# DeltaNet and an MLP on one core: hidden products of two feature pairs made for both token halves at once, and the last chunk's diagonal blocks turned on chip

## The chip, the cores and the metric

The kernel runs on one core of a Trainium2 chip. The metric is the device time of one execution in microseconds. Before the change, three runs gave 632.87 us as their median (630.61 to 633.9).

Engines are named as in the profile: PE is TensorE's matmuls and PEld its weight loads, DVE is VectorE, ACT is ScalarE, POOL is GpSimd, SP is SyncE, which here issues DMAs.

## The reference

Two operators follow each other. The first is a recurrence over 768 tokens for each of 4 x 8 heads of 48 dimensions, with a 48 x 48 state; keys are normalised, and `y` reads the state before the token is added to it. The second is an MLP over 3072 tokens: 384 features to 2048, `h * sigmoid(h)`, and back to 384.

```python
k_n = k / (np.linalg.norm(k, axis=-1, keepdims=True) + 1e-06)
for t in range(S):
    y[:, :, t] = np.einsum('bhd,bhde->bhe', q[:, :, t], state)
    v_old = np.einsum('bhde,bhd->bhe', state, kt)
    state = state + bt[:, :, :, None] * np.einsum('bhd,bhe->bhde', kt, vt - v_old)
x = attn_out.transpose(0, 2, 1, 3).reshape(B * S, H * D)
h = x @ w_in
g = h * (1.0 / (1.0 + np.exp(-h)))
return g @ w_out
```

## The kernel before, in words

**Tiling.** The 768 tokens are worked on in six chunks of 128 (`c` = 0 to 5), each in two halves of 64 tokens (`hf`). The four batches lie in two groups `g`. A half chunk of all batches is one column tile of 4 x 64 = 256 tokens for the MLP, kept in `xTs[c, hf]` as three K tiles of 128 features. Every matrix product in FP32 is recorded as two MATMUL instructions and two weight loads.

**The recurrence.** For each chunk the kernel scores keys against keys and queries (`score`, L526), inverts triangular 64 x 64 matrices, and then advances the state. The inverse begins with the 32 x 32 diagonal blocks of all heads, four to a head: each partition holds one block (block row by column in the free dimension), so that DVE can eliminate in 31 steps (`invert`, L645), each a SCALAR_TENSOR_TENSOR (L656) and a TENSOR_TENSOR (L661). Scores come out with token rows on the partitions, so the blocks must be rearranged. For chunks 2 to 5 this goes through DRAM: `block_out` (L598) stores eight times on SP, `block_in` (L609) loads once, and after the inverse `low` and `up` are stored and read back in place by `read_up` (L617) into `xe`, `xi` and `crossed`. For chunk 1 it stays on chip: `diagonal_blocks` (L564) copies the blocks together, `turn_diagonal` (L576) transposes them on DVE, and `put_up` (L630) transposes the result twice and copies it in place. `merge` (L793) completes the inverses with small matmuls; `keys`, `inner`, `old`, `update` and `new` (L850 to L949) advance the state and make `y`; `even_heads` and `move` (L953, L923) bring `y` into `xTs`, by ACT copies and five DMAs on SP.

**The MLP.** `hidden(c, hf)` (L1081) makes the 2048 hidden features in eight rounds `f`; each round makes two feature blocks of 128 (six products of 256 columns), with one PSUM bank of the two in `M`, emptied by one Silu activation on ACT. `combine(c, hf)` (L1185) multiplies with `w_out` in a 2 x 2 x 2 scheme of seven products instead of eight (Strassen's, in Winograd's form): seven chains of eight products with 192 columns, for which DVE makes sums of hidden rows (`sum_g`, L1175: S1, S2, S3, S4). For the last chunk alone `hidden_of_both` (L1261) makes the hidden products of both halves at once, with such a seven-product scheme over two feature blocks, two of the three K tiles, and the two token halves. It uses all eight banks, sums of `w_in` (`sum_w_in`) and of the tokens (`sum_x`) made on DVE, copies of partial results by ACT, and adds on DVE.

**The order.** Nothing is left to a planner: `pin` (L78) chains each engine's instructions in the order in which the program emits them, and `in_line` (L92) does so for the DMAs on SP. The MLP of chunk c runs while the recurrence of chunk c+1 is prepared and solved: `pieces` is a generator of MLP work, and a text for each chunk (L1656) tells how it is crossed with the rest. In such a text `r` takes the next MLP step (three products of hidden rows, or four of a chain), `s` the next step of `solve(c)`, `y` the next step of `prepare(c + 1)` (queries turned by `turn_blocks`, scores, blocks out and in), `i` one step of the inverse, `g` the step sizes for it, `v` and `k` loads, `d` the waiting output stores, `m` the next chunk's key lengths. So an `i` between two `r` puts DVE's step between these MLP steps' DVE instructions.

## Time and profile before

| | us |
|---|---|
| three runs, median (lowest to highest) | 632.87 (630.61 to 633.9) |
| the profiled execution's own time | 633.96 |
| span of its trace | 631.8 |

The trace holds one execution. Its span is the time from the first to the last instruction; the execution's own time lies 2.2 us above it. "Busy" is the time in which an engine worked on at least one instruction. The chain that ended last follows the work back from the last instruction to what released each step; its rows give a start, a duration and what ran. In the view of the timeline and of the groups, a row has the engine, the line, the operation, output and inputs by the program's names, the shapes, a count, and then the durations; in brackets stands the idle time before it and what ended it. In the table of stretches a row has the limits, the length, the busy time of PE, PEld, DVE, ACT and POOL with the number of instructions, the granted clock of TensorE, the share of the DMA engines and GB/s. Rows that name a source line give the least, median and greatest duration in ns.

In this trace the MLP of chunk 4 begins at 455.7 us, its first combination at 482.9, its second half's hidden products at 501.1, and the second combination at 521.9; chunk 5's recurrence lies across the latter from 527 to 555. The last chunk's hidden products end at 591.9.

### The profile page before, as it was taken

The numbers are of one execution on the slowest core, as the hardware profiler recorded it, in microseconds if no ns is written. First come the engines' busy times: TensorE is split into PE (matmuls) and PEld (weight loads), VectorE is DVE, ScalarE is ACT, GpSimd is POOL, SyncE is SP. The second block draws the span as 40 slices with busy tenths as digits, with TensorE's granted clock in tenths as the row PEclk, the third lists the DMA queues.
The fourth block names the chain that finished last, engine by engine and source line by source line (L and its number), as shares of the span: only waits on it lengthen the run. The fifth ranks groups of instructions, "written<-read, shape, count | busy, mean of one in ns | idle before, by whom it ended". The sixth has DMA issues, their size and how long they took to land.

```text
span 631.8 us, 21374 instructions
## 1 busy us (share of the span) xinstructions
PE 617.7 (98%) x9390; PEld 543.3 (86%) x9390; DVE 415.5 (66%) x927; ACT 226.7 (36%) x516; POOL 94.0 (15%) x101
## 2 busy tenths in 40 slices
PE   8889989999999999999999999999999999999997
PEld 5578778666799989989989989989989989988997
DVE  6886779999667974546975554976444983345432
ACT  4657873332441122451122451122452122454210
POOL 5234631335020020020020010020002000000000
PEclk9869999999999999999999999999999999999999
DMA  9656506350459360459141359433254024010011
GB/s 175 134 141 199 170 16 149 116 86 4 101 100 186 62 108 4 95 107 188 34 92 20 72 125 156 65 75 44 52 113 95 2 75 62 17 38 1 0 26 26
DMA packets 136941, 52.61 MB, mean 83 GB/s; under 512 B 108672, under 2 KB 130432, under 8 KB 136848
## 3 DMA queue, kind: packets, MB, share of 16 engines
q1 hardware_dynamic: 136512, 51.09, 39.6%
q8 instruction: 74, 1.21, 0.9%
q10 hardware_dynamic: 336, 0.15, 0.1%
q14 instruction: 19, 0.16, 0.1%
HBM read 39.09 MB, written 9.96 MB: 78 GB/s over the span
## 4 chain that ended last, share of the span: by engine, by line
PE 93%; SPq 2%; DMA 1%; issue 1%; ACT 1%; DVE 0%
PE phid L1088 34%; PE px L1200 17%; PE py L1200 13%; PE po L1132 5%; PE pb_c L866 3%; PE pa L539 2%; SPq L144 2%; PE pb_c L1303 2%; PE pb_c L854 2%; PE pyc L945 2%; PE pc L1303 2%; PE pb_c L1132 2%; PE pb_c L886 2%; PE pa L1303 1%; PE pyc L932 1%; PE px L808 1%
## 5 line engine op out<-in xcount | busy, mean ns | idle before, releaser
L1088 PE MATMUL phid<-xT,w_in 128*128 128x256 f32 x960 | 214.9, 382 | 1.9 <-issue 1.7
L1088 PEld LDWEIGHTS phid<-xT,w_in 128*128 128x128 f32 x960 | 180.2, 190 | 26.9 <-issue 2.8
L1098 ACT ACTIVATE gT<-phid 128x512 f32<-128x512 f32 x72 | 42.9, 597 | 115.2 <-PE phid L1088 106.2
L656 DVE SCALAR_TENSOR_TENSOR rank<-g,step,x 128x31 f32<-128x31 f32 (+15 forms) x124 | 49.8, 402 | 23.3 <-DMA g<-blocks 19.8
L1200 PE MATMUL px<-sums_of_w,sums_of_g 128*128 128x192 f32 x320 | 56.6, 329 | 0.0
L1200 PE MATMUL py<-w_out,sums_of_g 128*128 128x192 f32 x320 | 56.2, 328 | 0.0
L1200 PEld LDWEIGHTS px<-sums_of_w,sums_of_g 128*128 128x128 f32 x320 | 52.2, 190 | 0.4
L1200 PEld LDWEIGHTS py<-w_out,sums_of_g 128*128 128x128 f32 x320 | 52.3, 190 | 0.3
L661 DVE TENSOR_TENSOR x<-x,rank 128x31 f32<-128x31 f32 (+15 forms) x124 | 42.5, 342 | 4.3
L477 POOL TENSOR_TENSOR vf<-vf,n_slot 128x768 f32<-128x768 f32 x10 | 14.8, 1492 | 175.4 <-DMA vf<-in_v_dram 129.9
L1183 DVE TENSOR_TENSOR sums_of_g<-gT 128x384 f32<-128x384 f32 (+1 forms) x48 | 24.6, 540 | 14.6 <-ACT gT L1098 14.5
L498 DVE STREAM_TRANSPOSE kq<-stage 128x512 f32<-128x512 f32 x28 | 28.4, 1121 | 6.8 <-DMA stage<-in_q_dram 3.5
L554 ACT COPY xT<-pyc 48x128 f32<-48x128 f32 (+2 forms) x120 | 31.1, 259 | 1.6
L1211 DVE TENSOR_TENSOR o<-o,kept 128x192 f32<-128x192 f32 (+1 forms) x29 | 11.5, 425 | 26.7 <-ACT kept L1208 26.7
L560 POOL COPY g<-x 64x256 f32<-64x256 f32 x4 | 5.0, 1244 | 150.8 <-DVE x L664 150.8
L891 DVE TENSOR_TENSOR state<-state,pb_c 128x384 f32<-128x384 f32 x22 | 11.2, 550 | 24.6 <-PE pb_c L886 24.6
L866 PEld LDWEIGHTS pb_c<-vf,xi 64*64 64x64 f32 x736 | 23.3, 138 | 3.2 <-issue 2.3
L866 PE MATMUL pb_c<-vf,xi 64*64 64x48 f32 x736 | 24.9, 223 | 0.1
L1132 PE MATMUL po<-w_out,gT 128*128 128x384 f32 x64 | 23.7, 491 | 0.0
L1200 PE MATMUL py<-w_out,gT 128*128 128x192 f32 x128 | 23.4, 331 | 0.0
L859 DVE TENSOR_TENSOR vf<-vf,pb_c 128x384 f32<-128x384 f32 x22 | 11.2, 550 | 18.3 <-PE pb_c L854 15.5
L1200 PE MATMUL px<-w_out,gT 128*128 128x192 f32 x128 | 22.4, 327 | 0.0
(293 smaller groups left out, 1094.5 us busy)
## 6 DMA issues: line engine op xcount, KB each, us to landing
vf<-in_v_dram SPq DMA_DIRECT2D x48, 96.0 KB, 2.8
out_dram<-o SPq DMA_DIRECT2D x42, 96.0 KB, 2.2
w_out<-in_moe_w_in_dram SPq DMA_DIRECT2D x4, 768.0 KB, 5.0
sums_of_w<-in_moe_w_out_dram SPq DMA_DIRECT2D x4, 768.0 KB, 4.6
kb<-in_k_dram SPq DMA_DIRECT2D x12, 192.0 KB, 4.5
kb<-in_k_dram SPq DMA_DIRECT2D x24, 96.0 KB, 4.0
raw<-in_moe_w_in_dram SPq DMA_DIRECT2D x3, 768.0 KB, 6.8
blocks<-ap SPq DMA_DIRECT2D x32, 64.0 KB, 1.9
```

The lines of the kernel that those rows point to most:

```text
L477: pin(nc.gpsimd.tensor_tensor(out=vf, in0=vf, in1=of, op=ALU.mult))
L498: pin(nc.vector.transpose(out=kqs[c, b][:, :, j, :].rearrange("p a (i m) -> p a m i", i=T), in_=src.rearrange("p a (m d) -> p a m d", d=D) ...
L554: return pin(nc.scalar.copy(to, of))
L656: pin(nc.vector.scalar_tensor_tensor(out=tv, in0=g[:, 0:m, m : m + 1].to_broadcast([P, m, n]), scalar=step[:, m : m + 1], in1=x[:, m : m + ...
L661: yield pin(nc.vector.tensor_tensor(out=x[:, 0:m, m:T], in0=x[:, 0:m, m:T], in1=tv, op=ALU.add))
L866: yield pin(nc.tensor.matmul(pz[rows, n * D : (n + 1) * D], lhsT=xis[g][rows, u * H + 2 * p + e, :], rhs=vfs[c][rows, hf, g * HB + u, p, : ...
L1088: pin(nc.tensor.matmul(ph[:, j * GT : (j + 1) * GT], lhsT=w_in[:, a, (2 * f + j) * P : (2 * f + j + 1) * P], rhs=xTs[c, hf][:, a, :], star ...
L1098: pin(nc.scalar.activation(out=hidden_of(c, hf, f), in_=ph[:], func=ACTF.Silu, scale=-0.5 if in_blocks(c) else 0.5))
L1132: pin(nc.tensor.matmul(pos[i][:, 0:DM], lhsT=hidden_of(0, hf, f // 2)[:, at : at + C], rhs=w_outs[f // HFF][:, f % HFF, :], start=(f == 0) ...
L1183: pin(nc.vector.tensor_tensor(out=sums_of_g[:, k, fs], in0=of[0], in1=of[1], op=op))
L1200: pin(nc.tensor.matmul(to, lhsT=at, rhs=quarter(f, *b) if isinstance(b, tuple) else sums_of_w[b][:, f], start=start and f == 0, stop=f == ...
L1303: pin(nc.tensor.matmul(to[:, i * GT : (i + 1) * GT], lhsT=left(a, slice(f, f + 1))[:, 0], rhs=right(b), start=start and i == 0 and n == 0, ...
```

## The change

For chunk 4 (the second last), the features' rounds 0, 1, 3 and 4 are taken as two pairs (0,1 and 3,4: `TWOS[:2]`), each made for both token halves at once by the scheme that the last chunk has already, which now is a class `Both` with its steps as methods. Rounds 2, 5, 6 and 7 (`PLAIN`) stay as they were, made by `plain`. `some_of_both` runs the four plain rounds of the first half, then the two pairs, crossed with each other, on the two banks of `M` and one each of `A` and `CC`, and the second half's round 7 between them; then comes the combination of the first half, then `others` with the second half's rounds 2, 5 and 6, then the second combination. The sums of `w_in` for the two pairs are made here, on DVE, behind the first two of the last chunk's four turned queries and ahead of the other two; they stay for the last chunk, which now makes only those of rounds 2, 5, 6 and 7 itself. The second half's hidden rows of the pairs lie in `kbufs[0]` and `stage`.

For chunk 5, the diagonal blocks no longer go through DRAM: they are copied into the end of `stage` by ACT (six copies) and DVE (two), transposed on DVE, and put in place after the inverse by two DVE transposes and ten copies (`put_up`), as chunk 1 has it: six by ACT, two each by DVE and POOL. POOL clears `spread` once, as the blocks of chunk 5 have another place in it. The texts for chunks 4 and 5 are written anew.

```diff
+        if c == NCH - 1:
+            pin(nc.gpsimd.memset(spread[:], 0.0))
...
-        return 2 * (1 - j % 2) + j // 2 if c > 1 else j
+        return 2 * (1 - j % 2) + j // 2 if 1 < c < NCH - 1 else j
...
-            room = stage if c == 0 else sum_room
+            room = (stage, sum_room, stage[:, -BH * T :])[min(c, 2)]
...
+    def put_up(c, x):
...
         pin(nc.vector.transpose(out=both[:].rearrange("p n s -> p s n"), in_=x))
-        up = work.tile([P, BH, T], FP32, name="up_1", tag="x", bufs=1)[:]
+        if c > 1:
+            yield
+        if c == 1:
+            up = work.tile([P, BH, T], FP32, name="up_1", tag="x", bufs=1)[:]
+        else:
+            up = zbuf[:, HB:B].rearrange("p b s a w -> p (b s a w)").rearrange("p (n t) -> p n t", t=T)
         pin(nc.vector.transpose(out=up.rearrange("p n t -> p t n"), in_=x.rearrange("p s t -> p t s")))
+        if c > 1:
+            yield
...
-        if c == 1:
-            put_up(x)
+        if c in (1, NCH - 1):
+            yield from put_up(c, x)
             return
...
+    ALONE = slice(2, NFF // 2, FG)
+    TWOS = [slice(f, f + 2) for f in range(0, NFF // 2, FG)]
+    PLAIN = [*range(NFF // 2)[ALONE], *range(NFF // 2)[TWOS[-1]]]
+
+    def groups_of(c, hf):
+
+        if (c, hf) == (LAST - 1, 1):
+            return [*TWOS, ALONE]
...
+    def plain(c, hf, f):
...
+    def sum_w_in(fs):
+
+        w = lambda which: block_in_w(which, fs)
+        yield by_in(w(S_1), w((1, 0)), w((1, 1)), ALU.add)
+        yield by_in(w(S_2), w(S_1), w((0, 0)))
+        yield by_in(w(S_4), w((0, 1)), w(S_2))
+        yield by_in(w(S_3), w((0, 0)), w((1, 0)))
...
+        def first(self, f):
+
+            self.chain_of[f] = at, a = self.take("pa")
+            yield from self.products(a, f, ((0, 0), (0, 0)), start=True)
+            by_act(self.place(f, 0, 0), halves_of(a))
+            tag, b = self.take("pb")
+            yield from self.products(b, f, ((0, 1), (1, 0)), ((0, 2), (2, 0)), start=True)
+            self.add(self.place(f, 0, 0), b)
+            self.late.append(self.place(f, 0, 0))
+            self.free.append(tag)
...
+        def sums(self, f):
+            p = self.p[f][1]
+            yield from self.products(p, f, (S_1, 1), start=True)
+            by_act(self.place(f, 1, 1), halves_of(p))
+
+        def second(self, f):
+
+            a = self.chain_of[f][1]
+            yield from self.products(a, f, (S_2, 2))
+            by_act(self.place(f, 0, 1), halves_of(a))
...
+        def rest(self, f):
+            yield from self.products(self.d[f][1], f, ((1, 2), (2, 1)), start=True)
+
+        def third(self, f):
+
+            a, to = self.chain_of[f][1], self.place(f, 1, 1)
+            yield from self.products(a, f, (S_3, 3))
+            for of in (a, self.d[f][1]):
+                self.add(to, of)
+            silu(self.c, to, to)
+            self.free.append(self.d.pop(f)[0])
+
+        def fourth(self, f):
+
+            to = self.place(f, 0, 1)
+            yield from self.products(self.p[f][1], f, (S_4, (1, 1)), ((0, 2), (2, 1)))
+            self.add(to, self.p[f][1])
+            silu(self.c, to, to)
+            self.free.append(self.p.pop(f)[0])
+
+        def last(self, f):
+
+            at, a = self.chain_of.pop(f)
+            yield from self.products(a, f, ((1, 1), 4), ((1, 2), (2, 0)))
+            silu(self.c, self.place(f, 1, 0), halves_of(a))
+            self.free.append(at)
...
+    def some_of_both(c):
+
+        turns = zbuf[:, 0:HB].rearrange("p b s a w -> p (b s a w)").rearrange("p (k t) -> p k t", k=4)
+        both = Both(c, M, turns)
+        one, two = (fs.start for fs in TWOS[:2])
+        for f in PLAIN:
+            if f <= FG * (NG - 1):
+                room_for(f // FG)
+            yield from plain(c, 0, f)
+            if f == TWOS[-1].start:
+                together(sum_w_in(TWOS[0]), sum_w_in(TWOS[1]), both.sum_x())
+            yield
+        for which in (S1, S2):
+            sum_g(c, 0, which, NG - 1)
+        yield from both.first(one)
+        rooms = A.popleft(), CC.popleft()
+        both.free.extendleft(rooms)
+        yield from both.first(two)
+        both.begin(one)
+        yield from both.sums(one)
+        yield from both.second(one)
+        both.outputs()
+        yield from both.rest(one)
+        yield from both.fourth(one)
+        yield from both.third(one)
+        both.begin(two)
+        yield from both.second(two)
+        yield from both.sums(two)
+        yield from both.last(one)
+        for which in (S1, S2):
+            sum_g(c, 0, which, 0)
+        yield from both.rest(two)
+        yield from both.fourth(two)
+        yield from both.third(two)
+        yield from plain(c, 1, PLAIN[-1])
+        yield
+        yield from both.last(two)
...
-            if b % HB == 1:
+            if b % HB == 1 and c < NCH - 1:
                 block_out(c, b // HB)
...
-            block_in(c)
+            if c == NCH - 1:
...
+                    diagonal_blocks(c, 0, (by_act, by_act) * 2)
...
+                diagonal_blocks(c, 1, (by_act, by_dve) * 2)
+                yield
+                turn_diagonal(c)
...
-        4: "s2 r4 s r2 s r s r2 s r s r2 s r3 s2 d v y r3 g y r3 y r2 y r6 i r i2 r i2 r i r i r i3 r i r i2 r k i r i r i2 r2 i r i r i2 r i r i r i3 r i r i2 r i r i r m i2 r m3 r m4 r m4 r m4 r m4 r m4 r m4 r m4 r m4 r m4 m99",
-        5: "r s r2 s r s r2 s r s r s r s r2 s r s r2 s",
+        4: "s2 r4 s r2 s r s r2 s r s r2 s r3 s2 d v y r3 g y r3 y r4 y i r2 i r i r i2 r i r i r i r2 i r i2 r i r i r i r i r i r i2 r i r i r i2 r i r i2 r i r i r i2 r i r i2 r i r2 i r3 i r2",
+        5: "r2 s r2 s r s r2 s r s r s r s r s r s r2 s",
...
+            elif c < LAST:
+                pieces = chained(pieces, some_of_both(c), combine(c, 0), others(c), combine(c, 1))
```

More of the change, by code (lines that the diff above doesn't have):

```diff
@@ L1219, in steps @@
                 yield
[L1221 removed]
+        gs = range(len(groups_of(c, hf)))
         yield from steps(
[L1223 removed]
+            chain(px[:, left], (0, 0), (0, 0), True), *((s, g) for s in (S1, S2) for g in (
+                gs[1:2] if (c, hf) == (LAST - 1, 0) else gs if (c, hf) in ((LAST - 1, 1), (LAST, 1)) else gs[-1:]
+            ))
         )
@@ new lines, in halves_of, with hidden_of_both, seconds @@
+    def halves_of(t):
+        return t[:].rearrange("p (f t) -> p f t", f=2)
+    def hidden_of_both(c):
+        both = Both(c, (*M, *CC, *A), stage[:, 3 * NFF // 2 * P :].rearrange("p (k t) -> p k t", k=4))
+        def seconds(*fs):
+            for f in fs:
+                both.begin(f)
+            for f in fs:
+                yield from both.sums(f)
+            for f in fs:
+                yield from both.second(f)
+            both.outputs()
+            for step in (both.rest, both.third, both.fourth, both.last):
+                for f in fs:
+                    yield from step(f)
+        yield from both.first(0)
+        yield from both.first(2)
+        together(both.sum_x())
+        together(sum_w_in(ALONE))
+        yield from both.first(4)
+        yield from seconds(0, 2)
+        together(sum_w_in(TWOS[-1]))
+        yield from both.first(6)
@@ L1377, in feed_forward, with others @@
+    def others(c):
+        room_for(0)
+        flush()
+        for f in PLAIN[:-1]:
+            yield from plain(c, 1, f)
+            yield
     def feed_forward(c, hf):
```

201 lines of the change are left out of this document (86 added, 115 removed).

## The prediction

> **What bounds the kernel now.** I read the page first, then the table of stretches, the list of waits, and the chain that ended last. The page says that TensorE is busy all through, at full granted clock after the first slices, and that it carries the chain.
>
> ```profile
> span 631.8 us, 21374 instructions
> ...
> PE 617.7 (98%) x9390; PEld 543.3 (86%) x9390; DVE 415.5 (66%) x927; ACT 226.7 (36%) x516; POOL 94.0 (15%) x101
> ...
> PEclk9869999999999999999999999999999999999999
> ...
> PE 93%; SPq 2%; DMA 1%; issue 1%; ACT 1%; DVE 0%
> ```
>
> A busy TensorE need not be one at its peak, so I asked for the stretches around the change: hidden products of chunk 4's first half up to the end of its combination (455.60 to 500.98), the rest of chunk 4 with chunk 5's recurrence (500.98 to 554.91), and the last chunk's products. The second view is of all that TensorE waited for from 380 us to the end.
>
> ```profile
> 455.60:500.98 45.38, 45.38 (x471) 41.89 (x467) 26.54 (x60) 13.69 (x37) 3.95 (x4) 1.00 0.41 85
> 500.98:554.91 53.93, 53.69 (x1049) 48.56 (x1047) 29.87 (x66) 16.35 (x40) 1.25 (x1) 1.00 0.25 45
> ```
> ```profile
> PE px L808 <- issue: 0.2, 1, 0.2
> PE pyc L945 <- issue: 0.2, 1, 0.2
> ```
>
> Only 0.4 us of idle in a quarter of a millisecond, and none of it for data. So the DRAM round trip of the last chunk's blocks, which the change takes away, is already free; only fewer TensorE instructions can shorten the time, and any new wait of TensorE lengthens it one for one. The chain gives the price of each:
>
> ```profile
> 404.81 20.72 PE phid L1088 x96
> ...
> 471.77 0.25 PE pa L539
> ...
> 473.68 9.26 PE phid L1088 x42
> ...
> 527.06 1.22 PE py L808 x82
> ...
> 533.65 0.65 PE px L808 x48
> 534.30 0.24 issue
> 534.54 0.77 PE px L808 x52
> 535.31 1.50 PE px L1200 x8
> 536.81 1.30 PE py L1200 x8
> ...
> 556.47 3.45 PE pb_c L1303 x16
> ```
>
> A product of 128x128 by 256 columns is two instructions. Plain ones cost 20.72/96 = 0.216 us each, those of the seven-product scheme 3.45/16 = 0.216 us: the same. Eight instructions of a chain cost 1.30 us, and 1.50 behind the small matmuls of the recurrence, so each return from these costs about 0.2 us.
>
> **The terms on TensorE.** A pair of rounds needs 2 x 6 products for each half of the tokens, 24 in all. In the new scheme a round's two feature blocks, two of the three K tiles and the two halves form a 2x2x2 product of seven instead of eight: 11 for a round, 22 for the pair. I count them in the steps: first 2+4, sums 2, second 2, rest 2, third 2, fourth 4, last 4. Two pairs (rounds 0,1 and 3,4) are so treated, which saves 4 products = 8 instructions = 8 x 0.216 = 1.73 us. Rounds 2, 5, 6, 7 stay plain. Walking through the two scripts, the recurrence still interrupts chunk 4's products at the same places, after 18, 36 and 54 instructions, and chunk 5's scripts cut the chains eight times as before (the first cut comes after 40 chain instructions instead of 32). So the number of 0.2 us returns does not change: 0. Chain instructions: 0.
>
> **The terms elsewhere.** Removed: eight block stores on SP, one load back, one POOL and one DVE copy, and the stores and loads of the inverse. SP's issues behind them are output stores that nobody awaits: 0 us. Added on ACT: twelve block copies, and for each pair three copies and four activations where four activations stood. Added on DVE: eight adds, twelve sums, three transposes, four copies; on POOL a memset and two copies. Their prices (L664 is the inverse's scaling; it stays):
>
> ```profile
> L554 ACT COPY stage<-ap 32x512 f32<-32x512 f32 x6 | 3.7, 615 | 0.1
> ```
> ```profile
> L664 DVE TENSOR_TENSOR x<-x,step 128x1024 f32<-128x1024 f32 x4 | 4.9, 1224 | 0.1
> ```
> ```profile
> L634 DVE STREAM_TRANSPOSE xe_y<-sums_of_w x1: 1958/1958/1958, 134.9 to 134.9; 128x1024 f32<-128x1024 f32 x1
> ```
> ```profile
> L560 POOL COPY xi<-up 32x512 f32<-32x512 f32 x2 | 1.6, 776 | 8.5 <-DVE up L636 8.4
> ```
> ```profile
> 559.77 0.42 DVE L1277 TENSOR_TENSOR stage<-xT 128x256 f32<-128x256 f32 x1
> ...
> 561.76 0.69 DVE L1277 TENSOR_TENSOR kq<-kq,pb 128x512 f32<-128x512 f32 x1 [0.43 <-PE pb L1303]
> ```
>
> ACT gets 12 x 0.615 = 7.4 us of block copies and six more copies of about 0.6, 11 us in all, over 70 us in which it worked 30 of 99. DVE gets 8 x 0.69 + 12 x 0.42 + 3 x 1.96 + 4 x 0.6 = 18.8 us. Both fit on average, so what counts is where TensorE stands behind one of them in order. There are three such places.
>
> **Place 1, the sums.** They are issued after 36 product instructions, so behind the first two turned queries and ahead of the other two, which now wait behind them; behind those stand the masks of the scores, and TensorE waits for turned queries and masks.
>
> ```profile
> 461.60 2.02 DVE L498 STREAM_TRANSPOSE kq<-stage 128x512 f32<-128x512 f32 x2
> 465.10 2.18 DVE L498 STREAM_TRANSPOSE kq<-stage 128x512 f32<-128x512 f32 x2 [1.47 <-DMA stage<-in_q_dram]
> 467.50 0.42 DVE L549 TENSOR_TENSOR ap<-pa,above 128x256 f32<-128x256 f32 x1 [0.22 <-ACT ap L554]
> ```
> ```profile
> 462.76 3.18 SPq L925 DMA_DIRECT2D xT<-part  x5
> ```
> ```profile
> xT<-part SPq DMA_DIRECT2D x3, 48.0 KB, 2.2
> ```
>
> Two weight sums fit in before the sum of the tokens' second half must wait for its moves: issued from 462.76 on, 2.2 us to landing in the table of DMA issues, so the first is there at about 465.2. Nine more operations at 0.42 end at 469.0, the two transposes (2.02) at 471.0. The scores that need them began at 471.77 in the chain, 18 product instructions after the other scores, and still do: margin 0.8 us, so 0. If the moves landed 1.5 us later, this place would cost 0.7.
>
> **Place 2, the crossing of pair one, pair two and the inverse.** The products of pair one and two use two to four PSUM banks, so TensorE waits for ACT's copy and DVE's add before a bank is used again. After 473.68 TensorE has 148 - 54 = 94 instructions left up to the combination, 20.3 us. Pair one's "rest" product comes 26 instructions in, at 473.68 + 0.20 + 26 x 0.216 = 479.5, and overwrites the bank that the add of pair two must have read. ACT must first finish the scores' copies, then make six block copies, then that pair's copy:
>
> ```profile
> 474.00 0.38 ACT L554 COPY ap<-pb_c 128x256 f32<-128x256 f32 x1
> ```
>
> 474.4 + 6 x 0.615 + 0.6 = 478.7, add to 479.4, and about 0.2 us from the hand-over and from the bank being needed when the instruction starts rather than ends. TensorE waits some 0.3 us. From then on DVE has the block transpose 1.96, seven adds at 0.69, the first eight steps of the inverse and two sums of the hidden rows at 0.55, in order between the adds:
>
> ```profile
> 486.07 0.27 DVE L656 SCALAR_TENSOR_TENSOR rank<-g,step,x 128x31 f32<-128x31 f32 x1 [1.58 <-DMA g<-blocks]
> ...
> 491.66 0.43 DVE L656 SCALAR_TENSOR_TENSOR rank<-g,step,x 128x207 f32<-128x207 f32 x1
> ```
>
> Eight steps took 491.66 - 486.07 = 5.6 us, so the sum is 1.96 + 4.83 + 5.6 + 1.1 = 13.5 us, and TensorE wants the last add at 473.88 + 86 x 0.216 = 492.5, which is 13.6 us after DVE began at 478.9. DVE is full here. Placing the adds one by one, two hand-overs have less than 0.1 us to spare (the third product's add before the last products of pair one; the copy before the fourth products of pair two); I give each 0.1 us. Waits: 0.3 + 0.2 = 0.5 us. Lower bound 0 (a wait can't be negative, and none goes away). Upper bound: each of the seven adds stands behind a whole step, in the first case behind the transpose:
>
> ```profile
> L656 DVE SCALAR_TENSOR_TENSOR rank<-g,step,x 128x31 f32<-128x31 f32 (+15 forms) x31 | 12.5, 402 | 2.5 <-DMA g<-blocks 1.6
> L661 DVE TENSOR_TENSOR x<-x,rank 128x31 f32<-128x31 f32 (+15 forms) x31 | 10.6, 342 | 1.1
> ```
>
> 7 x 0.83 (0.402 + 0.342 and two gaps of 0.04) + 1.96 = 7.8 us. I take the value near the lower end, since the steps here are the short first ones and the written order puts most of them behind an add.
>
> **Place 3, the end of the inverse.** It starts some 4.5 us earlier (behind the transpose at 481.5, instead of 486.07). On DVE stand then 31 steps of 0.83 (25.7), six of the adds (4.1), the hidden rows' and outputs' sums of the first half (about 6), the scaling 1.22: it ends at 518.6, the two transposes at 520.5 and 522.5, ACT's six copies behind them at 526.2. Chunk 5's recurrence needs the first transpose at 473.9 + 20.3 + 112 x 0.1625 + 36 x 0.216 + 40 x 0.1625 = 526.7, and the copies a good 6 us later: margins of 6 us, so 0. The eight sums for chunk 4's second combination stand behind the second transpose; the first four end at 522.5 + 4 x 0.42 = 524.2 and are wanted at 525.4.
>
> One row of before speaks to that margin: a sum of hidden rows took twice its 0.55 us while POOL scaled vf.
>
> ```profile
> 476.26 2.91 POOL L477 TENSOR_TENSOR vf<-vf,n_slot 128x768 f32<-128x768 f32 x2 [53.80 <-DMA vf<-in_v_dram]
> 479.10 0.95 POOL L592 MEMSET x<- 128x1024 f32 x1
> ```
> ```profile
> 478.43 1.15 DVE L1183 TENSOR_TENSOR sums_of_g<-gT 128x384 f32<-128x384 f32 x1 [2.48 <-ACT gT L1098]
> 479.61 0.56 DVE L1183 TENSOR_TENSOR sums_of_g<-sums_of_g,gT 128x384 f32<-128x384 f32 x1
> ```
>
> POOL's two new copies (2 x 0.78 us) start with the same transpose's end as those eight sums. The Trainium skill, page "SBUF — State Buffer", section "Who interferes with whom", says that a VectorE instruction with two SBUF inputs and a GpSimd instruction that reads SBUF share a port, and that the later of the two is held until the other has ended; the 1.15 agrees with it. By that rule the sums would be held for up to 1.55 us against a margin of 1.2, and the total would come out 0.35 us higher than by the row of an undisturbed sum; the adds of place 2 take one input from PSUM and would not be held. That lies inside the forecast's own range, so it gets no chance of its own.
>
> **The sum.** -1.73 + 0.5 = -1.2 us. The profiled execution took 633.96 us around its span of 631.8, 0.2% above the median of 632.87; its span should become 630.6. From the median: 631.6 us, with its own range 631.1 (no waits) to 632.4.
>
> **The rivals.** (a) More is saved. Beside the matmuls, the chain has gaps that it calls "issue" and slow stretches of the recurrence:
>
> ```profile
> 460.61 0.95 PE pyc L945 x64
> ...
> 553.64 1.34 PE pyc L945 x64
> ```
>
> 0.39 us here, and 0.65 + 0.24 + 0.77 against 1.22 for an equal merge, 0.44, both near the block transfers that go. If these go as well and there is no wait: -1.73 - 0.83 = -2.6, 630.3 us. Against it: nothing ties the gaps to the transfers. (b) The waits at place 2 eat the gain, 1.2 to 2.4 us of them: 632.9, no change. For it speaks that DVE is full there; against it, that most adds come ahead of a step. (c) Slower: DVE becomes the bound at place 2 and TensorE follows it add by add, at worst 7.8 - 1.73 = +6.1, 639.0 us. It ends slower once the waits pass 1.73 us, and by more than 0.5% from 4.9 us. The full 13.5 us speak for it; against it, that TensorE has independent products (the plain round 7, the other pair) between most hand-overs.
>
> **How the numbers follow.** 0.5% (3.2 us) is about what a measurement of this kernel can tell from no change. Forecast 0.47, (a) 0.15, (b) 0.2, (c) 0.18. Forecast and (b) lie within 0.5%; (a) stays inside unless other noise adds to it, so two thirds of it; of (c) four fifths count as slower. Faster 0.1, same 0.75, slower 0.15. The range runs from 629.9, below (a), to 634.8, which takes in the lower part of (c).
>
> **What would show it.** Right: 184 instead of 192 plain-sized instructions in chunk 4's products, at 0.216 us; the last chunk's products (the run at 556.47) about 1.2 us earlier; waits of TensorE for DVE or ACT near 479 to 493 of about half a microsecond in all; no blocks, low and up transfers for the last chunk. Wrong: several gaps on TensorE in that stretch, ended by adds; turned queries after 471.8; a merge that waits for an ACT copy; or more 0.2 us returns than counted.

## The result, and the profile after

The changed kernel's time is 630.64 us (median of 20 runs, 628.97 to 633.68); the kernel before, on the same chip and beside it, took 631.14 us (20 runs, 630.37 to 635.13). The ratio is 0.9976 with a 95% interval of 0.9964 to 0.9987: 1.5 us faster, between 0.8 and 2.3 us. The forecast was 1.2 us faster (631.6 from 632.87, a ratio of 0.998), and it called that a difference which a measurement could not tell.

The page of the changed kernel answers to the one of before: eight TensorE instructions fewer (9390 to 9382), more work on DVE (415.5 to 429.1 us) and ACT (226.7 to 237.7 us). The profiled execution took 631.02 us around its span.

```profile
span 629.2 us, 21396 instructions
...
PE 614.6 (98%) x9382; PEld 540.3 (86%) x9382; DVE 429.1 (68%) x957; ACT 237.7 (38%) x534; POOL 94.6 (15%) x103
```

The span fell by 2.6 us, but not all of this comes from the change. The tables of stretches, cut at the same places of the program in both kernels, show where it went. The columns are the stretch, its length, then the busy time of TensorE, its weight loads, DVE, ACT and POOL. The rows are, in order: from chunk 4's first hidden product to its second combination; that combination with chunk 5's recurrence; the last chunk's hidden products; its combinations and the end. First before, then after.

```profile
455.60:521.70 66.10, 66.10 (x567) 60.14 (x563) 43.43 (x100) 18.20 (x45) 5.20 (x5) 1.00 0.35 76
521.70:552.08 30.38, 30.14 (x882) 28.06 (x880) 11.29 (x23) 10.78 (x30) 0.00 (x0) 1.00 0.28 40
552.08:591.70 39.62, 39.62 (x245) 34.67 (x241) 20.08 (x36) 18.60 (x35) 0.00 (x0) 1.00 0.07 16
591.70:631.79 40.09, 36.57 (x225) 36.27 (x223) 11.98 (x20) 4.55 (x12) 0.00 (x0) 1.00 0.09 21
```
```profile
454.46:519.25 64.79, 64.79 (x560) 58.37 (x555) 55.43 (x120) 25.26 (x57) 4.23 (x4) 1.00 0.23 50
519.25:549.29 30.04, 30.04 (x881) 28.06 (x879) 14.49 (x32) 14.50 (x36) 1.36 (x2) 1.00 0.04 10
549.29:588.67 39.38, 39.38 (x245) 34.49 (x241) 18.76 (x37) 18.62 (x35) 0.00 (x0) 1.00 0.07 16
588.67:629.16 40.49, 36.57 (x225) 36.27 (x223) 11.80 (x20) 4.56 (x12) 0.00 (x0) 0.98 0.08 20
```

The stretch in which the products were saved is 1.31 us shorter. The next two are shorter by 0.34 and 0.24 us, the last is 0.40 us longer although TensorE is busy for the same 36.57 us in it. What is left, 1.1 us, lies ahead of 455 us, where both kernels issue the same work but for POOL's one clearing of `spread`. That part moves by itself: it took 455.60 and 457.56 us in two executions of the kernel before, 454.46 and 455.02 us in two of the changed kernel. The third stretch took 39.38 us in the second execution of the kernel before, too, so the 0.24 us are not the change's either.

In the first stretch, 1.73 us of instructions went, and 0.42 us of waits came. The chain of the changed kernel at the crossing of the two pairs shows two of them: four instructions take 0.86 us where they wait for nothing, and 1.08 and 0.96 us in two places. The list of what the weight loads (PEld) waited for, from 470 to 495 us, names the cause: the sums (`pc`) and the rest (`pd`) of pair one wait for a DVE add (L1301). The weight loads stand ahead of the matmuls, so their waits (0.4 and 0.2 us) are longer than what the matmuls lost (0.22 and 0.10 us).

```profile
476.72 1.08 PE pc L1344 x4
477.81 0.86 PE pa L1344 x4
478.67 0.96 PE pd L1344 x4
```
```profile
PEld pc L1344 <- DVE gT L1301: 0.4, 1, 0.4
PEld pa L541 <- DVE ap L551: 0.3, 1, 0.3
PEld pd L1344 <- DVE gT L1301: 0.2, 1, 0.2
PEld pb L1344 <- ACT gT L1107: 0.2, 1, 0.2
```

The wait for the rest product had been foreseen, the one for the sums had not. A look at the copies of blocks on DVE (L559) and at POOL's scaling of the values (L479) beside them shows what made that add late. The figures behind "x2" are the shortest, median and longest duration in ns, then the first and last start.

```profile
L559 DVE COPY stage<-ap x2: 418/1012/1607, 473.9 to 474.3; 32x512 f32<-32x512 f32 x2
```
```profile
L479 POOL TENSOR_TENSOR vf<-vf,n_slot x2: 1568/1612/1655, 474.1 to 475.6; 128x768 f32<-128x768 f32 x2
```

The copy that started at 473.9 us, ahead of POOL, took 0.42 us; the equal one that started at 474.3 us, behind POOL's start, took 1.61 us. The add stands behind it.

### The profile page after: what moved, and what is told of

It reads as the page before. It is cut to its first block, busy times and chain, and to the rows that moved or that the text cites. A ratio compares the mean times of both kernels' runs of the same rounds, so it can differ in the third digit from the quotient of the medians.

```text
span 629.2 us, 21396 instructions
## 1 busy us (share of the span) xinstructions
PE 614.6 (98%) x9382; PEld 540.3 (86%) x9382; DVE 429.1 (68%) x957; ACT 237.7 (38%) x534; POOL 94.6 (15%) x103
## 4 chain that ended last, share of the span: by engine, by line
PE 94%; DVE 3%; issue 1%; DMA 1%; ACT 0%; SPq 0%; POOL 0%; POOLq 0%; DVEq 0%
PE phid L1118 30%; PE px L1234 17%; PE py L1234 13%; PE po L1166 5%; PE pb_c L1344 3%; PE pb_c L875 3%; PE pa L541 3%; PE pc L1344 2%; PE pa L1344 2%; PE pb_c L863 2%; PE pyc L954 2%; PE pb_c L1166 2%; PE pb_c L895 2%; PE pb L1344 1%; PE pyc L941 1%; PE px L817 1%
## 5 line engine op out<-in xcount | busy, mean ns | idle before, releaser
L1118 PE MATMUL phid<-xT,w_in 128*128 128x256 f32 x864 | 194.3, 382 | 0.8 <-issue 0.7
L1118 PEld LDWEIGHTS phid<-xT,w_in 128*128 128x128 f32 x864 | 161.9, 190 | 23.7 <-issue 1.9
L1107 ACT ACTIVATE gT<-phid 128x512 f32<-128x512 f32 x62 | 36.8, 597 | 95.6 <-PE phid L1118 88.4
L479 POOL TENSOR_TENSOR vf<-vf,n_slot 128x768 f32<-128x768 f32 x10 | 15.0, 1521 | 172.6 <-DMA vf<-in_v_dram 98.7
L1217 DVE TENSOR_TENSOR sums_of_g<-gT 128x384 f32<-128x384 f32 (+1 forms) x44 | 21.2, 508 | 6.5 <-ACT gT L1107 6.4
L541 PE MATMUL pa<-kq 48*64 48x128 f32 (+1 forms) x384 | 19.8, 255 | 2.5 <-ACT kq L522 1.4
L541 PEld LDWEIGHTS pa<-kq 48*64 48x64 f32 x384 | 18.0, 133 | 4.8 <-ACT kq L522 2.3
L562 POOL COPY g<-x 64x256 f32<-64x256 f32 x3 | 3.7, 1245 | 118.6 <-DVE x L673 118.6
```

The source lines that it names most:

```text
L541: pin(nc.tensor.matmul(pa[e][half, p * n * W : (p + 1) * n * W], lhsT=kq[rows, p, 0, half], rhs=kq[rows, p, js[0] : js[-1] + 1, half], sta ...
L1107: pin(nc.scalar.activation(out=to, in_=of, func=ACTF.Silu, scale=-0.5 if in_blocks(c) else 0.5))
L1118: pin(nc.tensor.matmul(ph[:, j * GT : (j + 1) * GT], lhsT=w_in[:, a, (2 * f + j) * P : (2 * f + j + 1) * P], rhs=xTs[c, hf][:, a, :], star ...
L1217: pin(nc.vector.tensor_tensor(out=sums_of_g[:, k, fs], in0=of[0], in1=of[1], op=op))
```

## The experiments

The theory to be tested: the gain is the four products less 0.4 us of waits; turning the blocks on chip gains nothing by itself. Its rivals: the gaps that the chain calls issue went with the block transfers; DVE is not really full at the crossing; the late copy is slow for a reason of its own. One kernel was not run: the pairs with the blocks still going through DRAM. So the gain of the products alone is worked out from the stretches, not measured by itself.

**The blocks alone.** Chunk 4's products are all plain; the blocks are turned on chip.

```diff
-            if c < LAST - 1:
+            if c < LAST:
                 pieces = chained(pieces, feed_forward(c, 0), feed_forward(c, 1))
-            elif c < LAST:
-                pieces = chained(pieces, some_of_both(c), combine(c, 0), others(c), combine(c, 1))
```

> The last chunk's blocks are turned on chip as after the change, but chunk 4's hidden products are all plain, as before it. Forecast (the DRAM round trip of the blocks was free, the gain is the four products): 0.0 us against the kernel before, at most 0.3 to either side, and chunk 4's products take as long as before. First rival (the issue gaps near the block transfers went with the transfers): 0.4 to 0.8 us faster than before, all of it in chunk 5's recurrence (the merge 1.32 instead of 1.66 us, the last `new` 1.09 instead of 1.34 us, as after the change). Second rival (the on-chip copies cost something): 0.3 to 1 us slower, seen as a wait of TensorE for ACT or DVE.

Measured: ratio to before 1.0016 (0.9996 to 1.0036). The same first two stretches of this kernel, and what TensorE waited for in the first:

```profile
454.86:522.30 67.44, 66.37 (x568) 60.06 (x563) 51.04 (x106) 23.47 (x54) 5.82 (x6) 1.00 0.22 47
522.30:553.03 30.73, 30.46 (x881) 28.10 (x880) 11.36 (x24) 12.79 (x34) 0.00 (x0) 1.00 0.04 10
```
```profile
PE phid L1111 <- ACT gT L1100: 1.1, 1, 1.1
```

The second rival holds, and by more than the 1 us that it allowed. The first stretch is 1.34 us longer than before, 1.1 us of it one wait: plain products have two PSUM banks, each emptied by one ACT operation, and that operation stood behind six block copies of 0.62 us. The recurrence (30.73 us) is no shorter than before (30.38 us, and 31.17 us in a second execution below). So the on-chip blocks gain nothing and, taken alone, cost more than the forecast's 0. In the changed kernel, with the same copies, the waits come to 0.42 us in all. That the two more banks of the pairs' scheme are the reason is likely, but no run isolates it.

**The kernel before, again.** Nothing is edited.

> The kernel before, unchanged, measured against itself, for what such a measurement can tell and for what moves in the trace when nothing is changed. If 0.5% is about what it can tell (as the forecast had it), the interval is some 0.5% wide to either side; the rival is that 20 executions tell 0.1%, so that a gain of 1.5 us (0.24%) stands out clearly. In the trace: if the gaps called issue in chunk 5's recurrence are noise, the merge and the last `new` differ by some 0.3 us from the first profile of the same kernel; if they belong to the transfers, they come again at 1.66 and 1.34 us.

Measured: ratio 1.0001 (0.9978 to 1.0024), with 12 runs against 35. The same four stretches but the third:

```profile
457.56:523.67 66.11, 66.11 (x569) 60.15 (x564) 43.57 (x100) 18.20 (x45) 5.20 (x5) 1.00 0.36 76
523.67:554.84 31.17, 30.41 (x882) 28.21 (x880) 11.28 (x23) 10.78 (x30) 0.00 (x0) 1.00 0.29 40
594.22:634.30 40.08, 36.56 (x225) 36.27 (x223) 11.98 (x20) 4.55 (x12) 0.00 (x0) 0.99 0.09 21
```

One program, two executions: the first stretch repeats to 0.01 us and so does the end, but the recurrence takes 31.17 us instead of 30.38. The third stretch, from 554.84 to 594.22 us, takes 39.38 us instead of 39.62, as long as in the changed kernel. What the chain calls issue in the recurrence changes from one execution to the next, and no gain can be read from it.

**The changed kernel, again.** Nothing is edited.

> The changed kernel unchanged, beside the third pair on the same chip, for the comparison and for what moves in its trace by itself. Expected: ratio to before 0.9976 within 0.2%, the stretch from chunk 4's first hidden product to its second combination 64.8 us to within 0.05, chunk 5's recurrence different by some tenths of a us if its gaps are noise, and the end behind the last TensorE instruction 3.9 us if it belongs to the program, 3.5 if it is chance.

Measured: ratio 0.9984 (0.9963 to 1.0004). Its stretches say the same: 64.79 us once more, the recurrence 31.03 instead of 30.04 us, the end 40.47 instead of 40.49.

```profile
455.02:519.81 64.79, 64.74 (x560) 58.45 (x555) 54.29 (x120) 25.16 (x57) 3.98 (x4) 1.00 0.25 50
519.81:550.84 31.03, 30.43 (x881) 28.24 (x880) 14.49 (x32) 14.48 (x36) 2.03 (x2) 1.00 0.04 10
590.22:630.69 40.47, 36.56 (x225) 36.27 (x223) 11.78 (x20) 4.55 (x12) 0.00 (x0) 1.00 0.08 20
```

In this execution POOL's scaling began only at 475.5 us, since the values landed later, and both block copies on DVE took 0.42 us. The wait ahead of pair one's sums was gone; the one ahead of its rest had grown (the four instructions took 1.13 us; 0.96 in the first execution, 0.86 without a wait), and the stretch was the same:

```profile
PEld pd L1344 <- DVE gT L1301: 0.5, 1, 0.5
```

What repeats of the change is therefore -1.31 us in the first stretch and +0.40 us at the end, together -0.9 us. That lies inside the measured interval, and this second timing has its middle at 1.0 us (with 12 runs its interval no longer excludes no change); the rest of the 1.5 us is not traced to the change.

**The transpose made twice.** DVE does 2.1 us more at the crossing, into the same place.

```diff
-        pin(nc.vector.transpose(
-            out=blocks[c][1].rearrange("p s t -> p t s"), in_=diagonals.pop(c).rearrange("p n t -> p t n")
-        ))
+        of = diagonals.pop(c)
+        for _ in range(2 if c == NCH - 1 else 1):
+            pin(nc.vector.transpose(out=blocks[c][1].rearrange("p s t -> p t s"), in_=of.rearrange("p n t -> p t n")))
```

> The changed kernel with VectorE's transpose of the blocks (2.11 us) made twice into the same place, so 2.1 us more of VectorE at the crossing of the two pairs. Forecast (VectorE is full there and TensorE follows it add by add): by the trace after, the add from pair one's sums bank would end at about 484.4 instead of 482.3 us, TensorE's next sums want that bank at 482.92 us, so a wait of about 1.5 us there and 0.2 more at the next bank: 1.7 us slower than the changed kernel, back at the time of the kernel before. Rival (the independent products cover it): less than 0.5 us slower than the changed kernel, with no wait over 0.2 us at pair two's sums.

Measured: the stretch takes 66.68 us instead of 64.79, 1.89 us more for 2.1 us of DVE work; ratio to before 1.0013 (0.9993 to 1.0033). The stretch, and TensorE's waits in it:

```profile
455.77:522.45 66.68, 65.24 (x560) 58.30 (x555) 56.22 (x121) 25.07 (x57) 3.95 (x4) 1.00 0.23 48
```
```profile
PE pc L1344 <- DVE kb L1301: 1.4, 1, 1.4
```

The wait is where it was forecast, at pair two's sums. DVE is full at the crossing, as the prediction worked out, with a few tenths to spare.

**The second batch group's block copies behind the first add.** The four copies of the blocks of batches 2 and 3 (two by ACT, two by DVE) come three steps of products later; the texts of the expectations call these blocks the second half's.

```diff
+                yield
                 diagonal_blocks(c, 1, (by_act, by_dve) * 2)
                 yield
...
-        4: "... y r3 y r4 y i ..."
+        4: "... y r3 y r3 y r1 y i ..."
```

> The changed kernel with the copies of the second half's blocks (two on ACT, two on VectorE) written out behind pair one's first add instead of ahead of it; nothing else moves. Reading of the trace after: the wait of 0.22 us ahead of pair one's sums (476.72) comes from that add, which stood behind a VectorE block copy of 1.61 us instead of 0.42, held up while GpSimd scaled the values. If so, the wait goes, the chain from the first hidden product of chunk 4 to its second combination is 0.2 us shorter (64.6 instead of 64.8 us), and a copy that starts while GpSimd is scaling still takes well over 0.42 us. Rival (the wait is the add's own hand-over, or the products would catch the other delay instead): the stretch stays 64.8 us, because pair one's rest product waits for ACT by as much more.

Measured: the stretch takes 64.47 us, 0.32 less than in the changed kernel; ratio to before 0.9972 (0.9947 to 0.9997). Both waits are gone: the same chain has 0.86 us for all three groups. The copy that started while POOL scaled took 1.61 us again, now where nobody waited for it.

```profile
476.12 0.86 PE pc L1344 x4
476.99 0.86 PE pa L1344 x4
477.85 0.86 PE pd L1344 x4
```
```profile
L559 DVE COPY stage<-ap x2: 418/1012/1606, 474.3 to 474.7; 32x512 f32<-32x512 f32 x2
```

**The scaling last.** POOL's scaling is written out behind the transpose; nothing else moves.

```diff
-            for g in range(2):
+            for g in range(2 if c < NCH - 1 else 0):
                 size(c, g)
...
                 turn_diagonal(c)
+                for g in range(2):
+                    size(c, g)
```

> The changed kernel with GpSimd's scaling of the last chunk's values (two of 1.6 us) written out behind the blocks' transpose instead of ahead of chunk 5's scores. Reading so far: VectorE's block copy of 1.61 us was held by that scaling. If so, both copies take 0.42 us, pair one's add is on time, the waits ahead of pair one's sums (0.22) and rest (0.10) go, and the operations of VectorE that now run beside the scaling, the first steps of the inverse with both inputs in SBUF, take up to 3.2 us longer in all; pair one's adds stand behind those steps, so up to 1.7 us of new waits at pair two's sums, as when the transpose was made twice: the stretch from chunk 4's first hidden product to its second combination between 64.5 and 66.2 us. Rival (the copy is slow for another reason, ACT reading the same rows beside it): it stays at 1.6 us with no GpSimd instruction beside it, and the stretch at 64.8 us.

Measured: both copies now take 0.42 us, and ACT still copies the same rows beside them, so POOL it was. But the stretch takes 64.78 us, as in the changed kernel; ratio to before 0.9993 (0.9973 to 1.0013). The scaling still ran from 475.4 to 478.3 us, ahead of the inverse, so the 3.2 us of held steps that the expectation allowed for did not come.

```profile
L559 DVE COPY stage<-ap x2: 416/420/424, 474.2 to 474.6; 32x512 f32<-32x512 f32 x2
```
```profile
476.83 0.61 ACT stage L556
...
477.47 0.59 ACT gT L556
...
478.09 0.70 DVE gT L1301
...
478.83 1.13 PE pd L1344 x4
```

The chain shows why: the wait for the sums is gone, and the whole delay is now at the rest product, behind ACT's sixth block copy, pair two's copy and the add. ACT's queue sets the end of this place, and DVE's late copy only moved part of the wait to an earlier instruction, as the two executions of the changed kernel have it. In the experiment before this one both waits went: there pair two's copy came ahead of two of ACT's block copies, and pair one's add ahead of DVE's two.

**A third pair.** Rounds 6 and 7 are also made for both halves. It takes eight banks instead of four; the second half's block copies come behind, and POOL's scaling beside the combination.

```diff
-    PLAIN = [*range(NFF // 2)[ALONE], *range(NFF // 2)[TWOS[-1]]]
+    PLAIN = [*range(NFF // 2)[ALONE]]
...
+        rooms = [*A, *CC]
+        both.begin(one)
+        both.begin(two)
+        yield from both.sums(one)
+        yield from both.second(one)
+        yield from both.sums(two)
+        yield from both.second(two)
...
+        both.begin(three)
+        yield from both.sums(three)
```

> The changed kernel with the third pair of rounds (6,7) of chunk 4 also made for both halves at once, eight PSUM banks instead of four for the products between the scores and the combination, the second half's block copies behind the scores' masks and two sums, and the scaling of the values late, beside the combination. Two products fewer, so 4 x 0.216 = 0.86 us less on TensorE, and the 0.4 us of waits of the change (ahead of pair one's first product, its sums and its rest) need not come: if the price per product of the forecast holds, the stretch from chunk 4's first hidden product to its second combination is 63.5 to 63.9 us instead of 64.8, and the time about 1 us below the changed kernel's, ratio to before about 0.996. Rival (VectorE is full at the crossing, and 4.4 us more of adds and sums stand there): waits of TensorE for adds of over 0.9 us, the stretch 64.8 us or more, no gain over the changed kernel.

Measured: slower than before, 1.0027 (1.0005 to 1.0049); the stretch takes 67.75 us, and TensorE waits 3.0 us in it, for two adds and for a copy of ACT that stood behind activations which waited for adds.

```profile
454.06:521.81 67.75, 64.59 (x556) 57.52 (x552) 57.41 (x127) 26.63 (x60) 4.01 (x4) 1.00 0.21 43
```
```profile
PE pb_c L1344 <- DVE kb L1301: 1.1, 1, 1.1
PE pa L1344 <- DVE stage L1301: 1.1, 1, 1.1
PE pa L1344 <- ACT stage L556: 0.8, 1, 0.8
```

**The third pair, with DVE relieved.** The weight sums of pairs two and three go to POOL, the sums of the hidden rows into the combination, the third pair's first products ahead, and some steps of the inverse behind. The cut of the diff is against the third pair's kernel.

```diff
-        together(sum_w_in(TWOS[1]))
+        together(sum_w_in(TWOS[1], in_by_pool))
...
+        together(sum_w_in(TWOS[2], in_by_pool))
...
-        4: "... y r3 y r3 y r1 y i r2 i r i r i2 r i r i r i r2 ..."
+        4: "... y r3 y r3 y r1 y r i r2 i r i r i r2 ..."
```

> The third pair again, with VectorE relieved where it kept TensorE waiting for 3.0 us before: the weight sums of pairs two and three (8 operations, 3.4 us) on GpSimd, the third pair's sums and second products written out ahead of pair two's third, so that ACT copies them before it waits for pair two's adds, the sums of the hidden rows in the combination, and some five steps of the inverse moved behind the adds. If VectorE's fullness was what ate the third pair's gain, the waits fall below 0.5 us and the stretch from chunk 4's first hidden product to its second combination is 63.4 to 64.3 us against 64.8 of the changed kernel, the ratio to before about 0.996. Rival (the work moved out of the crossing is missing later, or GpSimd's sums hold VectorE up on the way): the inverse ends after 525 us and the merge of the last chunk waits for the blocks' copies, or the sums come late; the stretch is 65 us or more, or the recurrence behind it grows by 1 us or more.

Measured: 1.0158 (1.0120 to 1.0196), much slower; the stretch takes 74.09 us. At the crossing TensorE waits 1.6 us instead of 3.0; 6.3 us of new waits stand at the two combinations, for the sums of hidden rows and for an activation. The rival's place was roughly right: the work that was moved out is missing later, at the combinations rather than at the merge (`issue` is a wait for nothing that the profile shows).

```profile
PE px L1234 <- ACT gT L1107: 4.1, 1, 4.1
PE px L1234 <- DVE sums_of_g L1217: 2.2, 1, 2.2
PE pb_c L1347 <- issue: 1.1, 1, 1.1
PE pa L1347 <- DVE stage L1301: 0.6, 1, 0.6
```

The chain ties the longest wait to the late inverse: its second transpose ended at 527.7 us, ACT's block copies behind it ran until 531.5, and only then came the activation for which the second combination waited (it went on at 532.15). Several things were moved at once here, so which move made the inverse late is open.

**Twelve more instructions on POOL.** For the 0.40 us at the end.

```diff
         if c == NCH - 1:
-            pin(nc.gpsimd.memset(spread[:], 0.0))
+            for _ in range(13):
+                pin(nc.gpsimd.memset(spread[:], 0.0))
```

> The changed kernel with GpSimd's clearing of the small spread tile made 13 times instead of once, early in chunk 3's stretch where GpSimd is idle: 12 instructions more in GpSimd's program, nothing else. The end behind TensorE's last instruction is 3.5 us in both profiles of the kernel before and 3.9 to 4.1 in all seven with the blocks turned on chip; in these, GpSimd pauses 0.35 us and SP 0.27 us among the last semaphore instructions, without waiting for data. If that belongs to where these instructions lie in the engines' programs, GpSimd's pause moves or goes (an end of 3.6 us) and SP's stays; the rival, that it comes with the transfers of the last outputs, leaves both as they are.

One execution took 632.11 us. Measured in its trace: the last stretch, from the last combinations' start, takes 40.19 us instead of 40.49; POOL's pause of 0.35 us among its last semaphore instructions is gone, SP's is there still. The rows give the first and last start of POOL's four last semaphore instructions (before, after, this run): 0.6, 0.9 and again 0.6 us apart.

```profile
590.09:630.28 40.19, 36.56 (x225) 36.26 (x223) 11.79 (x20) 4.56 (x12) 0.00 (x0) 0.99 0.09 20
```
```profile
L1792 POOLq EVENT_SEMAPHORE  x4: 17/17/17, 631.1 to 631.7; - x4
```
```profile
L1922 POOLq EVENT_SEMAPHORE  x4: 17/17/17, 628.2 to 629.1; - x4
```
```profile
L1923 POOLq EVENT_SEMAPHORE  x4: 17/17/17, 629.6 to 630.2; - x4
```

In two more kernels POOL's program is longer by at least twelve instructions, the third pair with its sums on POOL and the two gains together (below), and their ends have no such pause either; all other traces with the blocks on chip have it. So 0.30 us of the longer end hangs on POOL's program, and not on any data. The 0.10 us that is left comes with SP: the longest of its semaphore instructions at the end takes 28 ns before the change and 267 ns after it. Why, no run shows.

```profile
L1792 SPq EVENT_SEMAPHORE  x7: 17/28/28, 629.2 to 631.7; - x7
```
```profile
L1922 SPq EVENT_SEMAPHORE  x7: 17/28/267, 627.6 to 629.1; - x7
```

**The small gains together.** First the copies behind, timed again; then with the twelve memsets as well.

> The changed kernel with the second half's block copies behind pair one's first add, timed again with more rounds. If the two waits that went (0.32 us in the trace) are all there is, the stretch from chunk 4's first hidden product to its second combination is 64.47 us again, and the ratio to before some 0.0005 below the changed kernel's (0.9976 and 0.9984 so far), which lies inside the interval of 0.2%: the trace decides, the times should only not contradict it. Rival (a trade as with the scaling moved: one wait for another): 64.7 us or more.

> Both small gains found, together: the second half's block copies behind pair one's first add (two waits less, 0.32 us) and GpSimd's twelve extra memsets (its pause of 0.35 us at the end gone, 0.30 us). If both hold side by side, the stretch from chunk 4's first hidden product to its second combination is 64.47 us and the end from the last products' start 40.2 us, so 0.6 us less than the changed kernel apart from the recurrence's gaps, a ratio to before of about 0.997; the rival is that one undoes the other: 64.8 or 40.5 us again.

Measured: the copies behind give 64.47 us again (ratio 0.9985, 0.9962 to 1.0008); the two edits together give 64.46 and 40.20 us (0.9990, 0.9970 to 1.0009). In the trace the two gains stand side by side, 0.6 us below the changed kernel. The times neither confirm nor exclude that: their intervals are 1.2 to 1.5 us to either side, so the combination is not shown to beat the changed kernel.

## Why the prediction was right or wrong

**The bound, the saving, the returns: right.** TensorE stayed busy throughout, 8 instructions of 0.216 us went, and the first stretch shrank by that less the waits. With the blocks alone the recurrence was no shorter than before, so the DRAM round trip was free, as said.

**Place 1: right.** The changed kernel's trace reaches chunk 4 1.1 us earlier, so times are counted here from chunk 4's first hidden product (454.46 us; 455.60 before). The sums ended at 12.8 us (forecast 13.4), the last turned query at 14.8 (forecast 15.4), and the scores began at 16.2, as before. The 0 held.

**Place 2: the size right, the path half right.** Forecast 0.5 us, measured 0.31 (0.22 at the sums, 0.10 at the rest), plus 0.1 us within pair one's first products (the row above with ACT's `gT`), which was not in the forecast. The path through ACT's six copies was the one that set the end. What I had missed is that pair one's sums also stand behind an add, and that this add could stand behind a DVE copy that POOL holds up (in one execution of two it cost nothing in sum): I had said that the adds, with one input in PSUM, would not be held, and they were not, but a copy ahead of them was. The two tight hand-overs of 0.1 us each cost nothing. That DVE is full there was right: 2.1 us more of work gave 1.89 us more of time.

**The rule on the shared port.** The Trainium skill, page "SBUF — State Buffer", section "Who interferes with whom", says also that a VectorE copy can be in a mode in which it takes the ports that it shares with GpSimd, and that whichever engine was first keeps them for its whole instruction. The copy at 474.3 us agrees, 1.61 us against 0.42, and its return to 0.42 us once the scaling was moved. I had weighed only that section's sentence on two SBUF inputs, at place 3. There it agreed as well: two of the eight sums took 0.83 us instead of 0.41 beside POOL's copies (the longer one of the first row, and the second row), 0.8 us in all against my margin of 1.2, and TensorE did not wait.

```profile
L1217 DVE TENSOR_TENSOR sums_of_g<-kb x2: 401/618/834, 519.5 to 519.8; 128x256 f32<-128x256 f32 x2
...
L1217 DVE TENSOR_TENSOR sums_of_g<-stage x1: 825/825/825, 520.5 to 520.5; 128x256 f32<-128x256 f32 x1
```

**Place 3: right.** Counted in the same way, the inverse's scaling ended at 61.3 us (forecast 63.0) and ACT's last block copy at 69.4 (forecast 70.6), with no wait of TensorE.

**The end: missing from the sum.** Behind TensorE's last instruction the span runs on for 3.9 us instead of 3.5. I had put the removal of the stores and loads at 0 because nobody awaits what stands behind them; but the end is not only work, and pauses of SP and POOL among their last instructions added 0.40 us. The same 0.4 us came with the blocks alone (a last stretch of 40.50 us), so it belongs to the blocks' part of the change and not to the pairs.

**The rivals.** (a) falls: the gaps differ by 0.8 and 1.0 us between executions of one and the same program, and came again after the change. (b) and (c) did not come, but (c) was near: the third pair shows what happens when DVE's work goes past its room, 3.0 us of waits for 0.86 us saved.

**The step that failed** is the sentence that 0.5% (3.2 us) is about what a measurement of this kernel can tell from no change, and the chance of 0.75 for "same" that was built on it. The prediction shows no run for the 0.5%; the three single runs of before lie that far apart (630.61 to 633.9 us), but a median of many runs tells more than one run does. Twenty runs of each kernel gave an interval of 0.11% to either side, which excludes no change; with 12 runs it was about 0.2%, and the kernel before against itself gave 1.0001. So a gain of 1.2 us can be measured with twenty runs, and the forecast gave "faster" a chance of 0.1.

The mechanism held. In the sum one term was missing, the 0.40 us at the end, and the waits were 0.42 instead of 0.5 us: -1.73 + 0.42 + 0.40 = -0.9 us is what repeats in the traces, against the forecast -1.2. That 1.2 us lies inside the measured 0.8 to 2.3 us is therefore in part luck: the 0.6 us between what repeats and the measured middle of 1.5 us is traced to no part of the change.

## What to carry to other kernels

Judge a change of a few tenths of a per cent by the length of the stretch it touches: here that repeated to 0.01 us, while chunk 5's recurrence moved by 1 us from one execution to the next. Where an engine with room on average stands in order between two others, a wait that is removed at one instruction can come back whole at the next one; find the queue that ends last (here ACT's six copies) before moving the other. And ask of every operation ahead of a hand-over, not only of the hand-over's own, whether another engine can hold it up.

## What the runs showed of the hardware that was not expected

- A DVE copy of 32x512 within SBUF took 1.30 to 1.61 us instead of 0.42 when it began 0.2 to 0.5 us behind the start of a POOL multiplication of 128x768 values in SBUF, and ended 0.28 us after that multiplication. It was so in six traces: the changed kernel, both of the copies behind, the two gains together and both third pairs. Begun 0.1 to 0.3 us ahead of POOL, or with no POOL instruction beside it, the copy took 0.42 us.
- The end of the program, behind all data, took 0.4 us more after the change, and 0.30 of that went with twelve idle instructions on POOL. The Trainium skill, page "Runtime: NRT & Kernel Launch", section "Instruction fetch mechanics", says that an engine's instructions are fetched in blocks while it runs, and that this is mostly hidden. That these pauses are such fetches is a guess. The list of DMA transfers, which has a kind `instruction`, speaks for it: behind the span's end each trace with POOL's pause has two such transfers of 8 KB, each one without it a single one. It does not settle it, since the additional transfer starts 0.1 to 0.6 us after the span's end, behind the pause.
- The recurrence of the last chunk took 30.04 and 31.03 us in two executions of one program, with the granted clock at 1.00 in both. What TensorE lacked in these gaps, the trace does not tell.
